# Linear attention and an MLP-Mixer on one core: the second half of w_ch2 goes behind batch 1 in the stream of loads

## The chip, the cores and the metric

The kernel runs on one core of a Trainium2 chip. TensorE multiplies matrices, VectorE and ScalarE move and combine elements, GpSimd here mostly issues loads and stores, and 16 DMA engines move the data. The metric is the time on the device in microseconds (us), the median of three runs. Before the change it is 423.5 us (422.79 to 423.52). The profile is of one execution of 423.1 us, whose span from the first to the last instruction is 421.2 us; all times within the profile count from the start of that span.

## The reference

```
k_proj = E @ k            v_proj = F @ v          per batch and head, 1024 -> 64 rows
attn   = softmax(q @ k_proj.T / 8) @ v_proj       -> x, 1024 x 512 per batch
u      = x + (relu(x.T @ w_tok1) @ w_tok2).T      w_tok1 1024 x 256, w_tok2 256 x 1024
out    = u + relu(u @ w_ch1) @ w_ch2              w_ch1 512 x 1536, w_ch2 1536 x 512
```

There are 8 batches, 8 heads of 64, and a sequence of 1024. Inputs and output are float32; the products run in bfloat16 with float32 sums.

## The kernel before

The two channel products hold most of the work. A batch is cut into two blocks of 512 rows, so there are 16 blocks j. For each block `up_set` (from line 1127) computes relu(u @ w_ch1) in three sets, and `down_block` (from line 1218) multiplies the result, G, with w_ch2. Both use a scheme of Winograd and Strassen: a product of 2 x 2 quarters takes seven quarter products in place of eight, numbered 1 to 7, at the price of sums and differences of quarters on VectorE. Products 1, 2, 3 and 5 use quarters of the weights; products 4, 6 and 7 use combined quarters (`combine`, line 441: four differences a piece, of which number 5 overwrites a quarter of the weights). For w_ch2 (`wc2_sb`, combined in `wT2`) there are two pieces, chunks 0 to 2 and chunks 3 to 5 of each half of the 1536 rows. Every product of a down block runs over all six chunks, so no down-projection can start until both pieces of its quarter are there.

An up set is 7 products of 4 matmuls of 256 columns (line 1144). Between them ScalarE copies a partial sum from one PSUM bank into the next (line 1187), keeps two intermediate sums (line 1172) and applies two relus (line 1166), and VectorE makes two sums with relu (line 1125) and the four sums of G for the down block (line 1180). A down block is 14 groups of 6 matmuls of 256 columns (line 1253), with one ScalarE copy (line 1309) and six VectorE additions (lines 1293 and 1303).

Beside blocks 2b and 2b+1 runs the front of batch b+1: projections of K and V (`kv_proj`, lines 484 and 487), transposes of K and Q, scores with an exp on ScalarE (lines 597 and 606), attention (line 620, with VectorE at 632 and 637), then the two token products. For batch 1 the projections and the transposes are done in two halves of four heads each, on TensorE. G and S have two buffers each, by the parity of the block; K, V and Q have one each, so batch b+1 is loaded as batch b's projections leave them.

The order of instructions is computed, not written. Each piece of work is a job with an engine, an estimated duration, its dependencies and a due time, `prio`. `Planner.plan` (line 83) runs through estimated time: of the jobs that can start first on an engine it takes the one with the earliest due time, gives PSUM banks to those that need them (the up-projections may hold 5 of 8 banks at once, the down-projections 3, the front 3), and notes a start `j.start` and a place `j.at`. At the end all jobs are sorted by `at` and written out in that order, and `pin` ties each engine to it. So each engine runs its instructions in a fixed order, and an instruction that waits holds up all that follow it on its engine.

The loads are one stream in the planner, as fast as 0.40 MB of float32 a microsecond. All are issued by GpSimd, and convert to bfloat16. A load is marked `early`: its place is not its planned start but the moment at which its buffer is free (line 172), so it's issued well ahead, and waits its turn in the DMA queue. The loads of the beginning get their due times from a counter, `first`, in the order of the program: K, V, Q of batch 0 with w_tok1 among them, w_tok2, the six pieces of w_ch1, the four of w_ch2 (lines 384 to 390), and then K, V, Q of batch 1 (lines 1454 to 1456). This line decides the place in the order:

```
j.at = est[j.n] if j.early else t
```

Of the kernel before, what the change touches and what calls it, by code (L numbers as in the profile page):

```python
# [11 lines left out]
ALU = mybir.AluOpType  # L12
ACT = mybir.ActivationFunctionType
EARLY = 12.0
WHOLE = 3
TWO = 2
SUMS = 60.0
# [27 lines left out]
class Planner:  # L45
# [37 lines left out]
    def plan(self):  # L83
# [7 lines left out]
        for g in self.groups:  # L91
            first = min(j.prio for j in g)
# [8 lines left out]
        est = {}  # L101

        def open_(j):
            est[j.n] = max((d.end + self.LAG[d.eng] if d.eng != j.eng else d.full for d in j.deps), default=0.0)
            can.setdefault(j.eng, []).append(j)
# [14 lines left out]
        def home(b, now):  # L120

            if held[b.stream] + b.span > self.caps[b.stream]:
                return None
            if b.span == 2:
                free2 = [
                    (max(now, bank_free[i], bank_free[i + 1]), i) for i in PAIRS[b.stream]
                    if bank_free[i] is not None and bank_free[i + 1] is not None
                ]
                return (*min(free2)[:1], 0, 0, min(free2)[1]) if free2 else None
            if b.stream in "UD" and turn[b.stream][0] is not b:  # L130
                return None
            best = None
            keep = [i for i in self.homes["U"] if clean[i] and bank_free[i] is not None]
            if all(clean[:5]):
                keep = []
            for i in self.homes[b.stream]:
                t = bank_free[i]
                if t is None or (b.seeded and not clean[i]):
                    continue
                if not b.seeded and clean[i] and keep and keep[-1] == keep[0] == i:  # L140
                    continue
                c = (max(now, t), clean[i], t, i)
                if best is None or c < best:
                    best = c
            return best

        while any(can.values()):
            pick = None
            for e, js in can.items():
                f = free.get(e, 0.0)  # L150
                cands = []
                for j in js:
                    t = max(f, est[j.n])
                    spot = None
                    if j.takes:
                        h = home(j.takes[0], t)
                        if h is None:
                            continue
                        t, spot = h[0], h[3]
                    cands.append((t, j.prio, j.n, j, spot))  # L160
                if not cands:
                    continue
                t0 = min(c[0] for c in cands) + 0.02
                c = min((c for c in cands if c[0] <= t0), key=lambda c: (c[1], c[2]))
                if pick is None or c[0] < pick[0]:
                    pick = c
            if pick is None:
                raise RuntimeError("no job can go on", [(j.eng, j.fn.__qualname__, j.prio) for js in can.values() for j in js][:20], held, bank_free)
            t, _, _, j, spot = pick
            can[j.eng].remove(j)  # L170
            j.start, j.end, j.full = t, t + j.lat, t + j.lat + 0.03
            j.at = est[j.n] if j.early else t
            free[j.eng] = t + j.occ
            if j.takes:
                b = j.takes[0]
                b.at = spot
                turn[b.stream].remove(b)
                held[b.stream] += b.span
                for i in range(spot, spot + b.span):
                    bank_free[i] = None  # L180
            for b in j.banks:
                left[id(b)] -= 1
                if not left[id(b)]:
                    held[b.stream] -= b.span
                    for i in range(b.at, b.at + b.span):
                        bank_free[i] = max(x.end for x in b.jobs) + 0.1
                        clean[i] = b.full
            order.append(j)
            for s in j.next:
                waiting[s.n] -= 1  # L190
                if not waiting[s.n]:
                    open_(s)
# [6 lines left out]
def kernel(  # L199
# [16 lines left out]
    B, H, S, D = q.shape  # L216
# [121 lines left out]
    def ld(mb, fn, **kw):  # L338
        t = mb / 0.40
        j = pl.add("DMA", t, t + 2.0, fn, **kw)  # L340
        j.early = True
        return j


    def dma(dst, src):
        return lambda: nc.gpsimd.dma_start(out=dst, in_=src)  # L346
# [8 lines left out]
    def load_heads(b, name, h, hn, due):  # L355
        dst, src = {"k": (k_sb, k), "v": (v_sb, v), "q": (q_sb, q)}[name]
        hs = slice(h, h + hn)
        return ld(
            0.262 * hn,
            dma(dst[:, hs], src[b, hs].rearrange("h (p si) d -> p h si d", p=P)),  # L360
            writes=[(name, i) for i in range(h, h + hn)], prio=due,
        )
    first = iter(range(-1000, 0))
# [10 lines left out]
    for m in range(SETS):  # L374
        cs = slice(m * cw, (m + 1) * cw)
        for ch in range(2):
# [5 lines left out]
                writes=[("w1", m, ch)], prio=next(first),  # L382
            )
    w2_v = moe_w_ch2.rearrange("(ch cc p) d -> p ch cc d", ch=2, p=P)
    for c in range(0, C2, 3):
        for ch in range(2):
            ld(
                0.786, dma(wc2_sb[:, ch, c : c + 3], w2_v[:, ch, c : c + 3]),
                writes=[("w2", ch, c // 3)], prio=next(first),
            )  # L390


    TU = 24.65
# [77 lines left out]
    def kv_proj(b, h0, hn, due, block=False):  # L471
        hs = slice(h0, h0 + hn)
        hk = slice(h0 % (H // 2), h0 % (H // 2) + hn)
        heads = range(h0, h0 + hn)
        bk = Bank(stream[0], full=False)

        def view():
            return bank(bk).rearrange("p (h d) -> p h d", d=D)

        def mm(lo, hi):  # L480
            t = view()
            for si in range(lo, hi):
                a, z = si == 0, si == NSI - 1
                nc.tensor.matmul(  # L484
                    t[0:KP, 0:hn], ET_sb[:, si, :], k_sb[:, hs, si, :], start=a, stop=z
                )
                nc.tensor.matmul(
                    t[KP : 2 * KP, 0:hn], FT_sb[:, si, :], v_sb[:, hs, si, :], start=a, stop=z
                )

        cols = hn * D
        reads = ["ET", "FT"] + [(n, h) for n in "kv" for h in heads]
        pl.add(
            "PE", 8 * max(cols, 128) / 2400 + 0.22, 8 * max(cols, 128) / 2400 + 0.22,
            lambda: mm(0, NSI), reads=reads, takes=[bk], prio=due,
            after=[("vb", i, h) for i in range(2) for h in heads],
        )
        src = [lambda: view()[0:KP, 0:hn], lambda: view()[KP : 2 * KP, 0:hn]]
        if block:
            k_to = [kb[i * KP : (i + 1) * KP, hs, i, :] for i in range(2)]  # L500
        else:
            k_to = [kp[:, hk, i, :] for i in range(2)]
        v_to = [vb[i * KP : (i + 1) * KP, hs, i, 0:D] for i in range(2)]

        def copy(to, n):
            return lambda: nc.scalar.copy(out=to, in_=src[n]())

        for i in range(2):
            act(cols, copy(k_to[i], 0), writes=[("kb" if block else "kp", i, h if block else h % (H // 2)) for h in heads], uses=[bk])
        for i in (1, 0):  # L510
            act(cols, copy(v_to[i], 1), writes=[("vb", i, h) for h in heads], uses=[bk])

    def k_transpose_dma():
        sp(
            2.5,
            lambda: nc.sync.dma_start_transpose(
                out=kT.rearrange("p h c k -> p h (c k)"), in_=kb.rearrange("p h r d -> p (h r d)")
            ),
            reads=[("kb", i, h) for i in range(2) for h in range(H)],
            writes=[("kT", i, h) for i in range(2) for h in range(H)], prio=None,  # L520
        )
# [887 lines left out]
    def front(b, begin, end):  # L1409
        units = []  # L1410

        def unit(cost, f):
            units.append((cost, f))

        hn = H // 2 if b == 1 else H
        for i in range(H // hn):
# [3 lines left out]
            else:  # L1420
                unit(1.9, lambda t: kv_proj(b, 0, H, t - EARLY, True))
                unit(0.0, lambda t: k_transpose_dma())
# [7 lines left out]
        for h in range(H):  # L1430
            if h + 2 < H:
                unit(0.4, lambda t, h=h: scores(h + 2, t))
            if b >= WHOLE:
                unit(0.5, lambda t, h=h: attend_whole(h, t))
# [18 lines left out]

    for hh in range(0, H, H // 2):
        for name in "kvq":
            load_heads(1, name, hh, H // 2, next(first))
    for b in range(B):
        for j in (2 * b, 2 * b + 1):
            s_sums(j)
# [67 lines left out]
```

The softmax here doesn't subtract the row's maximum and nothing guards it: scores larger than these inputs give would overflow.

## Time and profile before

| What | Value |
|---|---|
| median of 3 runs | 423.5 us |
| span in the profile | 421.2 us |
| TensorE busy | 412.1 us |
| VectorE busy | 348.0 us |
| ScalarE busy | 231.8 us |
| GpSimd busy | 66.2 us |
| first up-projection starts | 32.3 us |
| first down-projection starts | 44.1 us |
| first K and V projection of batch 1 | 47.3 us |

Busy times overlap, and each is to be read against the span. A busy TensorE is not yet one at its peak: the end of a matmul is modelled and reaches into the next one, so a gap is better read from the starts of two neighbours and the known pitch. In the lines of the profile, L1253 is a line of the kernel, PE is a matmul, PEld a weight load, DVE VectorE, ACT ScalarE and POOL GpSimd. "psum<-wc_sb,G" names what is written and read, with numbers of buffers left out: wc_sb stands for the weights of both channel products and wT for their combinations.

### The profile page before, as it was taken

How to read it: one execution, taken by the hardware profiler on the slowest of the kernel's cores; microseconds unless marked ns; L12 is line 12 of the kernel's file. 1: busy time of each engine (PE TensorE's matmuls, PEld its weight loads, DVE VectorE, ACT ScalarE, POOL GpSimd, SP SyncE). 2: the span in 40 equal slices, each digit the busy share in tenths (PEclk: the TensorE clock that was granted, in tenths of full speed). 3: DMA queues.
4: the chain of work that ended last, by engine and by line, in shares of the span. 5: the costliest groups of instructions: out<-in, count | busy, mean ns of one | idle time of the engine just before them, and what ended most of it. 6: DMA issues, size and time to landing. Idle time of an engine off the chain costs nothing.

```text
span 421.2 us, 9421 instructions
## 1 busy us (share of the span) xinstructions
PE 412.1 (98%) x3838; PEld 347.7 (83%) x3838; DVE 348.0 (83%) x747; ACT 231.8 (55%) x444; POOL 66.2 (16%) x104
## 2 busy tenths in 40 slices
PE   7999999999999999999999999999999999999996
PEld 3587877688788888888798888888898899988885
DVE  2359969679679798988889899898988798997685
ACT  1858884475636546564645556655646645354530
POOL 8453220022003030022103020212100000010110
PEclk9999999999999999999999999999999999999999
DMA  9999999996975989398974989999760501250223
GB/s 166 207 201 206 207 206 164 225 177 140 216 145 103 195 133 235 64 186 141 207 163 94 191 139 224 163 200 179 153 146 0 152 27 76 50 151 2 102 100 103
DMA packets 96668, 62.48 MB, mean 148 GB/s; under 512 B 62064, under 2 KB 92272, under 8 KB 96624
## 3 DMA queue, kind: packets, MB, share of 16 engines
q0 software_dynamic: 34944, 45.09, 54.5%
q1 hardware_dynamic: 61056, 16.00, 21.6%
q10 hardware_dynamic: 624, 0.79, 0.7%
q8 instruction: 30, 0.49, 0.5%
q14 instruction: 14, 0.11, 0.1%
HBM read 59.24 MB, written 16.78 MB: 180 GB/s over the span
## 4 chain that ended last, share of the span: by engine, by line
PE 91%; DVE 4%; ACT 2%; DMA 1%; issue 0%; DVEq 0%
PE psum L1253 34%; PE psum L1144 33%; PE psum L848 4%; PE psum L484 4%; PE psum L597 3%; PE psum L964 3%; PE psum L656 2%; DMA o<-in_F_dram 1%; PE psum L620 1%; DVE u L1071 1%; PE psum L736 1%; PE psum L687 1%; PE psum L581 1%; PE psum L405 1%; PE psum L711 1%; PE psum L1032 1%
## 5 line engine op out<-in xcount | busy, mean ns | idle before, releaser
L1253 PEld LDWEIGHTS <-G 128*128 128x128 bf16 x1344 | 130.6, 98 | 19.7 <-issue 1.5
L1253 PE MATMUL psum<-wc_sb,G 128*128 128x256 bf16 x768 | 102.5, 273 | 0.5 <-ACT psum L1309 0.2
L1166 ACT ACTIVATE G<-psum 128x512 bf16<-128x512 f32 x96 | 57.3, 600 | 56.0 <-PE psum L1144 55.4
L1144 PEld LDWEIGHTS <-wc_sb 128*128 128x128 bf16 x768 | 73.8, 98 | 10.9 <-issue 0.6
L1253 PE MATMUL psum<-wT,G 128*128 128x256 bf16 x576 | 77.7, 273 | 0.1
L1180 DVE TENSOR_TENSOR G<-G 128x512 bf16<-128x512 bf16 (+1 forms) x140 | 69.5, 516 | 1.0
L1144 PEld LDWEIGHTS <-wT 128*128 128x128 bf16 x576 | 55.7, 98 | 9.0 <-issue 1.2
L1144 PE MATMUL psum<-uT,wc_sb 128*128 128x256 bf16 x384 | 57.7, 273 | 0.2 <-ACT psum L1187 0.2
L1144 PE MATMUL psum<-S,wc_sb 128*128 128x256 bf16 x384 | 57.6, 273 | 0.1
L1144 PE MATMUL psum<-S,wT 128*128 128x256 bf16 x384 | 55.6, 273 | 0.4 <-DVE S L781 0.4
L1287 POOL DMA_DIRECT2D out_dram<-o x30 | 16.4, 548 | 240.2 <-DVE o L1293 125.6
L1125 DVE CUSTOM_DVE_ANT_0 G<-psum,ub 128x512 bf16<-128x512 f32 x48 | 32.9, 685 | 15.3 <-PE psum L1144 15.1
L1172 ACT COPY ua<-psum 128x512 f32<-128x512 f32 x48 | 28.2, 588 | 30.1 <-PE psum L1144 29.7
L606 ACT ACTIVATE a<-psum 128x512 bf16<-128x512 f32 x64 | 36.4, 602 | 12.4 <-PE psum L597 11.8
L1293 DVE TENSOR_TENSOR o<-psum,u 128x512 f32<-128x512 f32 x55 | 37.5, 683 | 6.4 <-PE psum L1253 6.3
L1187 ACT COPY psum<-psum 128x512 f32<-128x512 f32 x48 | 27.8, 580 | 18.9 <-DVE G L1125 9.9
L1125 DVE CUSTOM_DVE_ANT_0 G<-psum,ua 128x512 bf16<-128x512 f32 x48 | 32.7, 682 | 5.0 <-ACT ua L1172 4.6
L1172 ACT COPY ub<-psum 128x512 f32<-128x512 f32 x48 | 28.2, 588 | 7.0 <-PE psum L1144 6.3
L1144 PE MATMUL psum<-uT,wT 128*128 128x256 bf16 x192 | 28.8, 273 | 0.1
L673 DVE TENSOR_TENSOR x_sb<-psum,rdn 128x512 bf16<-128x512 f32 x40 | 27.4, 686 | 0.6
L597 PE MATMUL psum<-qT,kT 128*128 128x512 bf16 x64 | 21.5, 380 | 0.6 <-ACT kT L549 0.6
L346 POOL DMA_DIRECT2D v_sb<-in_v_dram x18 | 13.5, 749 | 50.7 <-DMA uT<-u 48.0
(108 smaller groups left out, 547.2 us busy)
## 6 DMA issues: line engine op xcount, KB each, us to landing
out_dram<-o POOLq DMA_DIRECT2D x30, 512.0 KB, 4.2
k_sb<-in_k_dram POOLq DMA_DIRECT2D x14, 512.0 KB, 8.5
v_sb<-in_v_dram POOLq DMA_DIRECT2D x14, 512.0 KB, 10.3
q_sb<-in_q_dram POOLq DMA_DIRECT2D x14, 512.0 KB, 9.9
wc_sb<-in_moe_w_ch_dram POOLq DMA_DIRECT2D x6, 256.0 KB, 12.3
wc_sb<-in_moe_w_ch_dram POOLq DMA_DIRECT2D x4, 384.0 KB, 12.3
k_sb<-in_k_dram POOLq DMA_DIRECT2D x4, 256.0 KB, 6.8
v_sb<-in_v_dram POOLq DMA_DIRECT2D x4, 256.0 KB, 7.3
```

The costliest lines, as they stand in the source:

```text
L484: nc.tensor.matmul(t[0:KP, 0:hn], ET_sb[:, si, :], k_sb[:, hs, si, :], start=a, stop=z)
L597: lambda: nc.tensor.matmul(bank(bk), kT[:, h].rearrange("p c k -> p (c k)"), qT[:, h].rearrange("p j s -> p (j s)"), start=True, stop=True,),
L606: lambda: nc.scalar.activation(out=a_t[h // 2 % 2][:, h % 2], in_=bank(bk), func=ACT.Exp, scale=scale),
L673: lambda: nc.vector.tensor_tensor(out=x_sb[:, :, h * D : (h + 1) * D].rearrange("p (n c) d -> p n c d", n=2), in0=view()[:, :, :, 0:D], in ...
L1125: nc.vector._custom_dve(TENSOR_ADD_SAT, out=out, in0=in0, in1=in1, s0=FMAX, s1=0.0)
L1144: nc.tensor.matmul(t[:, c, :], w1_of(n, dd, 2 * m + c), a_of(j, n, dd), start=(n in (1, 7) and c == 0 and dd == 0), stop=(c == 1 and dd == 1),
L1166: lambda: nc.scalar.activation(out=G[:, n, cs], in_=view(src), func=ACT.Relu),
L1172: 512, lambda: nc.scalar.copy(out=dst, in_=view("y")), writes=[(name, s % 2)],
L1180: 512 * len(both), lambda: f(out=G[:, n, c], in0=G[:, a, c], in1=G[:, b, c]), ps=False,
L1187: 512, lambda: nc.scalar.copy(out=view("y"), in_=view("x")), takes=[bk["y"]],
L1253: nc.tensor.matmul(to, G[:, G_OF[n], cc, t * P : (t + 1) * P], w2_of(n, cc), start=(n in opens and (t == 0 or alone) and cc == 0), stop=(c ...
L1293: 512, lambda: nc.vector.tensor_add(out=dst, in0=view(src), in1=u_of(sh, dh)),
```

## The change

The load of w_ch2 is cut in two in time. Chunks 0 to 2 stay where they were in the stream, behind w_ch1. Chunks 3 to 5 go behind all loads of batch 1. The aim is that K, V and Q of batch 1 come earlier, while the first down-projections, which need all six chunks, come later. To this end the loads get due times by hand: -700 for the first half of w_ch2, -400 to -358 for batch 1, -340 for the second half. The second half isn't `early` any more; it gets a place of 16 us (in the planner's time) ahead of its planned start, which puts it behind the loads of batch 1 in GpSimd's order too.

```diff
+W2_DUE = (-700, -340)
...
-            j.at = est[j.n] if j.early else t
+            j.at = est[j.n] if j.early else t - 16 if -500 < j.prio < -300 else t
...
     for c in range(0, C2, 3):
         for ch in range(2):
             ld(
                 0.786, dma(wc2_sb[:, ch, c : c + 3], w2_v[:, ch, c : c + 3]),
-                writes=[("w2", ch, c // 3)], prio=next(first),
-            )
+                writes=[("w2", ch, c // 3)], prio=W2_DUE[c // 3] + 0.1 * ch,
+            ).early = W2_DUE[c // 3] < -500
...
     for hh in range(0, H, H // 2):
         for name in "kvq":
-            load_heads(1, name, hh, H // 2, next(first))
+            load_heads(1, name, hh, H // 2, -400.0 + 10 * hh + "kvq".index(name))
```

## The prediction

> **What bounds the kernel now.** I read the page first (busy shares, slices, chain), then the list of waits of TensorE, then a table of stages, then the timelines of TensorE and GpSimd between 30 and 60 us.
>
> ```profile
> PE 412.1 (98%) x3838; PEld 347.7 (83%) x3838; DVE 348.0 (83%) x747; ACT 231.8 (55%) x444; POOL 66.2 (16%) x104
> ...
> DMA  9999999996975989398974989999760501250223
> ...
> PE 91%; DVE 4%; ACT 2%; DMA 1%; issue 0%; DVEq 0%
> ```
>
> TensorE is busy for 98% of the span and is 91% of the chain that ended last. The DMA engines are full in the first nine slices, some 95 us less a dip. So the time is TensorE's work plus TensorE's holes, and the change alters no product: it can only open or close holes. The list of waits of TensorE says how many there are to close.
>
> ```profile
> PE psum L433 <- DMA o<-in_F_dram: 1.5, 1, 1.5
> PE psum L405 <- DVE zero L309: 1.0, 1, 1.0
> PE psum L597 <- ACT kT L549: 0.6, 2, 0.4
> PE psum L1085 <- DVE u L1071: 0.5, 1, 0.5
> PE psum L1144 <- DVE S L781: 0.4, 1, 0.4
> PE psum L1253 <- ACT psum L1309: 0.2, 1, 0.2
> ```
>
> All but the last lie before 36 us. A busy share hides part of a hole, because the modelled ends of matmuls overlap (a product of 4 shows 0.60 us but the next starts 0.44 us later). So I also took the starts in TensorE's timeline and subtracted the pitch of each group (0.109 us a matmul of 256 columns, 0.22 of 512, 0.057 of 128): some 2.0 us of holes between 26 and 41 us, 0.8 from 40 to 60, 0.3 from 60 to 80, 0.8 from 80 to 100, and 2.6 from 100 to the end. About 0.2 to 0.3 us of these comes with each K and V projection, wherever it stands.
>
> The stage that matters is the one in which the first down-projections run:
>
> ```profile
> 40.00:44.00 4.00, 3.89 (x37) 3.40 (x35) 4.00 (x11) 3.51 (x7) 0.00 (x0) 1.00 1.24 206
> 44.00:47.00 3.00, 3.00 (x30) 2.68 (x29) 3.00 (x7) 2.38 (x6) 0.00 (x0) 1.00 1.24 207
> 47.00:52.00 5.00, 5.00 (x62) 4.03 (x60) 5.00 (x13) 3.88 (x9) 2.02 (x3) 1.00 1.24 207
> 52.00:56.00 4.00, 4.00 (x40) 3.13 (x39) 3.82 (x12) 3.64 (x7) 0.20 (x1) 1.00 1.24 206
> ```
>
> The columns are the stretch, its length, then busy time of PE, PEld, DVE, ACT and POOL, the clock, the DMA share and GB/s. From 44 to 56 us VectorE is full (11.8 of 12.0 us), ScalarE works 9.9 of 12.0, and the DMA runs at its limit. All four resources are near their ends at once, and TensorE has no hole only because it has a third kind of work:
>
> ```profile
> 44.14 0.82 PE L1253 MATMUL psum<-wc_sb,G 128*128 128x256 bf16 x6
> ...
> 46.11 0.82 PE L1253 MATMUL psum<-wc_sb,G 128*128 128x256 bf16 x6
> ...
> 51.43 0.82 PE L1253 MATMUL psum<-wT,G 128*128 128x256 bf16 x6
> ...
> 52.96 0.82 PE L1253 MATMUL psum<-wT,G 128*128 128x256 bf16 x6
> ...
> 53.83 0.82 PE L1253 MATMUL psum<-wT,G 128*128 128x256 bf16 x6
> ...
> 54.82 0.82 PE L1253 MATMUL psum<-wT,G 128*128 128x256 bf16 x6
> ```
>
> These six groups of down block 0 are 6 x 0.655 = 3.9 us of TensorE work, and they ask almost nothing of the other engines: one ScalarE copy (L1309, 46.96 us) and one VectorE add (L1293, 53.81 us) in those 12 us.
>
> **What the Trainium skill says.** "Perfetto Trace Analysis", Identifying the Most-Contended Engine, warns that matmul busy time is a poor measure of headroom; the trace agrees (0.60 us shown, 0.44 us pitch), hence the pitch count above. "PSUM — Partial Sum Buffer", Engine vs sequencer instructions, says that ScalarE and VectorE queues are strict FIFO and matmuls start in program order. The trace fits: at 35.93 us TensorE stands still for 0.41 us for one S sum, although other products follow. So an early place in the order that proves too early costs everything behind it. "DMA: Bandwidth & Descriptors", Issuing engines are not separate DMA queues, says that all issuers share the same 16 engines: what goes ahead in the stream pushes back the rest. Its Bandwidth section measures 425 GB/s for a large load; here 206 GB/s land as bf16, which is 412 GB/s of float32 read, so the stream has no speed in hand.
>
> **The change, part by part.**
>
> 1. *Where the loads land.* The half of w_ch2 that moves is two pieces of 384 KB (as landed): 2 x 0.393 MB / 206 GB/s = 3.8 us. A load of four heads is 0.524 MB, 2.5 us; six of them are 15.3 us. The first projection of batch 1 shows when its V has come:
>
> ```profile
> 47.29 0.30 PE L484 MATMUL psum<-k_sb,ET_sb 128*64 128x256 bf16 x1
> 47.49 0.27 PE L487 MATMUL psum<-v_sb,FT_sb 128*64 128x256 bf16 x1
> ...
> 50.09 1.07 PE L581 MATMUL psum<-ident,q_sb 128*128 128x128 bf16 x16
> ```
>
>    V's first matmul trails K's by 0.2 us, and the Q transposes follow 2.6 us later, one load's time: this front runs as its data lands. So K, V, Q of heads 0 to 3 land at about 44.9, 47.4, 49.9 now, and at 41.1, 43.6, 46.1 after; heads 4 to 7 at 48.7, 51.2, 53.7 instead of 3.8 us later; and the two pieces of w_ch2 at 55.7 and 57.6 instead of about 40.4 and 42.3. Batch 2's loads are behind all of these either way and don't move. The issue on GpSimd costs 0.74 us a load, before and after alike, and the batch 1 loads would be issued some 3 us sooner into buffers that the batch 0 projections (done at 23.4 us) and transposes (24.4 us) have left, so nothing new holds them: zero.
>
> 2. *The four W2 combinations of that half* (L444, 128x768, 0.55 us each, pitch 0.46) leave a full VectorE between 43 and 52 us and return after 57.6 us, where it has room (1.84 of 4.00 us from 56 to 60). That takes 4 x 0.46 = 1.8 us off VectorE in the stage. TensorE gains nothing from it directly, since it had no hole there.
>
> 3. *Down block 0.* Every product runs over all six chunks, so its first needs the piece that lands at 55.7, and the second (from combined weights) 57.6 + 0.46 = 58.1 us. The six groups, 3.9 us, lose their place in 44 to 56 us. What can fill it? Up-projections of block 1: 11 of its 21 products are done later than 58 us now, so there is plenty, but a set of seven (7 x 0.44 = 3.06 us) asks ScalarE for five passes at 0.49 pitch, 2.45 us, and VectorE for two add-relus, 1.2 us, and four sums, 1.34 us, which can wait. ScalarE's 2.1 spare us would carry at most 2.1 x 3.06 / 2.45 = 2.6 us of these. Or batch 1's attention, 3.8 us sooner: for four heads TensorE 1.1 + 0.2 + 0.9 + 0.9 + 0.9 = 4.0 us against ScalarE 1.35 + 0.73 + 1.93 + 1.96 = 6.0 us. Filling with that costs 1.5 us of ScalarE for 1 of TensorE, so 2.1 us carry 1.4. Thus 3.9 us of filler is lost, and 1.4 to 2.6 us is the most that replaces it: a hole of 1.3 to 2.5 us. Bounds: 0 if the 1.8 us freed on VectorE and the three free D banks let the up sets run denser than now, 3.9 if nothing fills. I take 1.7, below the middle, because up-projections stand ready from 36 us on and ScalarE idles here mostly in pieces of 1 us that they can use.
>
> 4. *Afterwards.* From 58 us on the postponed block is a stock of light work (9.2 us on TensorE), and batch 1's front is up to 3.8 us ahead. That can close the holes between 60 and 100 us, 1.1 us less 0.4 that the projections bring, so 0.7. It cannot give back the hole of step 3, because TensorE was full from 58 to 80 already.
>
>    Sum: + 1.7 - 0.7 = + 1.0 us: 423.5 + 1.0 = 424.5 us.
>
> **The rivals.** *A: fillers suffice.* No net change, 423.5. For it: 11 products in stock, banks free. Against: ScalarE is 4.96 of 5.00 busy from 50 to 55 us even now. *B: faster, 422.5.* VectorE's relief and the earlier front close what can be closed: 0.7 from step 4 and some 0.3 of the holes from 40 to 60, with none opened. For it: every piece of the front is now used as it lands. Against: TensorE is not waiting for the front. *C: nothing fills and the order frays*, all 3.9 us lost: 427.4. For it: the FIFO queues; against: the stock of ready work.
>
> **How the numbers follow.** Forecast 0.50, A 0.25, B 0.17, C 0.08. The predicted time is the forecast's. Within the forecast the hole runs from 1.3 to 2.5 and the return from 0 to 0.7, so + 0.6 to + 2.5; about a sixth of it lies under the 0.85 us that count as a difference. That part and most of A make 0.30 for no change; 0.50 slower (0.42 forecast and C's 0.08); B and a little of A 0.20 faster. The range 422.4 to 426.6 takes in B's value and the forecast and leaves out C and tails.
>
> **What would show it.** Step 1: the first L487 of 256 columns near 43.6 us. Step 2: no second round of 128x768 combinations before 57 us. Step 3: no L1253 before 55.5 us; ScalarE above 11 of 12 us from 44 to 56; TensorE's holes of one to two and a half us there, waiting for ScalarE or VectorE. Step 4: fewer holes from 60 to 100. The prediction is wrong if TensorE stays without holes from 44 to 56, or if it has other holes after 100 us that a different order closes or opens.

## The result and the profile after

The changed kernel takes 425.22 us, the median of 4 runs (424.94 to 425.33), against 423.51 before (422.79 to 424.21): ratio 1.0039, 95% interval 1.0022 to 1.0057, so 1.7 us slower. In a second comparison, beside other kernels, it was 425.71 against 423.56: 1.0049, 1.0036 to 1.0062.

The page after, the same rows as before:

```profile
PE 413.0 (98%) x3838; PEld 347.3 (82%) x3838; DVE 347.6 (82%) x747; ACT 231.5 (55%) x444; POOL 66.1 (16%) x104
...
DMA  9999999994994989497998996795972511250223
...
PE 80%; DVE 8%; ACT 5%; DMA 4%; issue 1%; POOL 1%; POOLq 0%; DVEq 0%; ACTq 0%
```

In the profiled execution the span grew from 421.2 to 423.4 us while the work of VectorE and ScalarE stayed as it was. The chain that ended last now passes more often through the other engines: TensorE has 80% of it, against 91% before. TensorE's last group starts at 418.87 us in place of 416.38. To see where these 2.5 us come in, I took the pitch count of the prediction on both traces (start of the next group less the start of this one, less the pitch of this one's matmuls):

| holes of TensorE, us | before | after |
|---|---|---|
| 0 to 40 us | 11.2 | 11.5 |
| 40 to 64 us | 1.0 | 2.6 |
| 64 to 80 us | 0.3 | 0.2 |
| 80 to 100 us | 0.8 | 1.0 |
| 100 us to the end | 2.8 | 3.3 |

The 0.3 us of the first row is not the change: the first up-projection starts at 32.33 us before and at 32.64 after, but at 32.36 in a second profile of the changed kernel. Most of the change is in the second row. Before, this stage is one row of the table of stages (stretch, length, busy PE, PEld, DVE, ACT, POOL, clock, DMA share, GB/s):

```profile
44.00:64.00 20.00, 20.00 (x213) 16.39 (x212) 16.72 (x45) 16.89 (x34) 4.44 (x6) 1.00 1.24 207
```

and after:

```profile
52.00:56.00 4.00, 4.00 (x53) 3.15 (x51) 3.82 (x12) 3.94 (x10) 1.48 (x2) 1.00 1.24 205
56.00:60.00 4.00, 3.78 (x34) 2.81 (x32) 2.38 (x9) 3.95 (x8) 0.74 (x1) 1.00 1.23 205
60.00:64.00 4.00, 3.72 (x36) 2.94 (x35) 3.93 (x13) 3.32 (x7) 0.00 (x0) 1.00 1.25 208
44.00:56.00 12.00, 11.95 (x135) 9.34 (x130) 11.35 (x29) 11.57 (x26) 3.74 (x5) 1.00 1.24 206
44.00:64.00 20.00, 19.45 (x200) 15.09 (x195) 17.67 (x49) 18.85 (x39) 4.48 (x6) 1.00 1.24 206
```

The fourth number after the length is ScalarE: 18.85 of 20 us, up from 16.89, and 3.95 of 4 from 56 to 60 us, where TensorE loses time. TensorE's timeline after shows the holes one by one, and where down block 0 (L1255 in this kernel) now begins:

```profile
56.66 0.82 PE L1255 MATMUL psum<-wc_sb,G 128*128 128x256 bf16 x6
...
58.08 0.82 PE L1255 MATMUL psum<-wc_sb,G 128*128 128x256 bf16 x6
58.82 0.39 PE L622 MATMUL psum<-vb,a 128*128 128x130 bf16 x4
59.32 0.38 PE L599 MATMUL psum<-qT,kT 128*128 128x512 bf16 x1
59.80 0.60 PE L1146 MATMUL psum<-S,wc_sb 128*128 128x256 bf16 x4
60.23 0.39 PE L622 MATMUL psum<-vb,a 128*128 128x130 bf16 x4
60.79 0.38 PE L599 MATMUL psum<-qT,kT 128*128 128x512 bf16 x1 [0.17 <-ACT a L608]
61.28 0.82 PE L1255 MATMUL psum<-wc_sb,G 128*128 128x256 bf16 x6
```

Four matmuls of 130 columns take 0.23 us, but 58.82 to 59.32 is 0.50; a score takes 0.22, but 59.32 to 59.80 is 0.48. From 58.8 to 61.3 us there are four holes of 0.26 to 0.33, 1.1 us together. ScalarE's timeline has the other side of them:

```profile
57.76 1.01 ACT L591 COPY qT<-psum 128x1024 bf16<-128x1024 bf16 x1
58.67 0.60 ACT L608 ACTIVATE a<-psum 128x512 bf16<-128x512 f32 x1
59.16 0.59 ACT L1174 COPY ua<-psum 128x512 f32<-128x512 f32 x1
59.62 0.63 ACT L1168 ACTIVATE G<-psum 128x512 bf16<-128x512 f32 x1
60.11 0.63 ACT L608 ACTIVATE a<-psum 128x512 bf16<-128x512 f32 x1
60.59 0.65 ACT L1311 COPY psum<-psum 128x512 f32<-128x512 f32 x1
61.10 0.64 ACT L1168 ACTIVATE G<-psum 128x512 bf16<-128x512 f32 x1
```

There is no pause between any two: Q copies, exps, the passes of the up sets, and in their midst the one copy of the down block (L1311). Each of the four holes ends some 0.05 us after one of these does: at 59.27 (an exp), 59.75 (a copy of an up set), 60.74 (an exp) and 61.24 us (the down block's copy, after which its third group starts at 61.28). So even the filler that has come back stands in ScalarE's queue.

### The profile page after: what moved, and what is told of

The parts are those of the page before. It is cut to its first block, busy times and chain, and to the rows that moved or that the text cites. A ratio compares the mean times of both kernels' runs of the same rounds, so it can differ in the third digit from the quotient of the medians.

```text
span 423.4 us, 9409 instructions
## 1 busy us (share of the span) xinstructions
PE 413.0 (98%) x3838; PEld 347.3 (82%) x3838; DVE 347.6 (82%) x747; ACT 231.5 (55%) x444; POOL 66.1 (16%) x104
## 4 chain that ended last, share of the span: by engine, by line
PE 80%; DVE 8%; ACT 5%; DMA 4%; issue 1%; POOL 1%; POOLq 0%; DVEq 0%; ACTq 0%
PE psum L1255 32%; PE psum L1146 29%; PE psum L850 4%; PE psum L966 3%; DMA q_sb<-in_q_dram 3%; PE psum L486 3%; PE psum L599 2%; PE psum L658 2%; DVE G L1127 2%; DMA v_sb<-in_v_dram 2%; DVE G L1182 1%; DVE u L1073 1%; ACT qT L591 1%; PE psum L713 1%; PE psum L689 1%
## 5 line engine op out<-in xcount | busy, mean ns | idle before, releaser
L1255 PEld LDWEIGHTS <-G 128*128 128x128 bf16 x1344 | 130.2, 98 | 20.1 <-issue 2.3
L1255 PE MATMUL psum<-wc_sb,G 128*128 128x256 bf16 x768 | 102.7, 273 | 0.8 <-DVE wait L1295 0.4
L1255 PE MATMUL psum<-wT,G 128*128 128x256 bf16 x576 | 77.7, 273 | 0.2
L1146 PEld LDWEIGHTS <-wT 128*128 128x128 bf16 x576 | 55.5, 98 | 9.4 <-issue 1.0
L1146 PE MATMUL psum<-S,wc_sb 128*128 128x256 bf16 x384 | 57.6, 273 | 0.2
```

What stands on the lines that cost most here:

```text
L1146: nc.tensor.matmul(t[:, c, :], w1_of(n, dd, 2 * m + c), a_of(j, n, dd), start=(n in (1, 7) and c == 0 and dd == 0), stop=(c == 1 and dd == 1),
L1255: nc.tensor.matmul(to, G[:, G_OF[n], cc, t * P : (t + 1) * P], w2_of(n, cc), start=(n in opens and (t == 0 or alone) and cc == 0), stop=(c ...
```

## The experiments

The theory was: moving the load makes down block 0 late, TensorE loses its light work between 44 and 56 us, and ScalarE can't carry enough of the other work. The rivals were that the early front of batch 1 itself crowds ScalarE, and that a reshuffled order loses time anywhere. Holes are from the pitch count. In the table, the times of before are those measured beside each kernel, and "holes" are of TensorE. They are of one execution each, the times are medians: e7, for one, ran between 425.63 and 430.11 us, and its profile is of 428.76. A dash marks a trace that lacks a dozen matmul records, where a missing record would be counted as a hole.

| kernel | us | before beside it | ratio (95%) | holes 40 to 64 | 64 to 100 | after 100 |
|---|---|---|---|---|---|---|
| before | | | | 1.0 | 1.0 | 2.8 |
| after | 425.22 | 423.51 | 1.0022 to 1.0057 | 2.6 | 1.2 | 3.3 |
| e2, down block 0 held | 428.35 | 423.44 | 1.0099 to 1.0134 | 2.7 | 0.6 | 5.7 |
| e3, half not loaded | 426.85 | 423.44 | 1.0058 to 1.0095 | 1.4 | 0.9 | 5.2 |
| e4, after without Q copies | 425.61 | 423.44 | 1.0037 to 1.0062 | 1.1 | 2.3 | 3.7 |
| e5, before without Q copies | 423.89 | 423.44 | 1.0002 to 1.0018 | 0.6 | 1.4 | 3.9 |
| e1, half way | 428.11 | 423.45 | 1.0091 to 1.0127 | 1.3 | 1.7 | 6.4 |
| e6, e3 with a clean start | 423.92 | 423.45 | 1.0002 to 1.0021 | 0.9 | 1.0 | 3.9 |
| e7, short hold | 427.45 | 423.45 | 1.0065 to 1.0126 | 1.2 | 0.6 | 8.1 |
| e8, e2 without Q copies | 426.50 | 423.45 | 1.0057 to 1.0112 | 0.9 | 3.4 | 3.0 |
| e9, after, Q copies on VectorE | 431.84 | 423.56 | 1.0176 to 1.0219 | - | - | - |
| e10, before, Q copies on VectorE | 429.83 | 423.56 | 1.0119 to 1.0169 | - | - | - |
| e11, one load later | 423.53 | 423.56 | 0.9991 to 1.0007 | - | - | - |

**e2: the late block without the moved load.**

```diff
-        product(1, 0)
+        opening[j] = product(1, 0)[0]
...
+    opening[0].deps.add(proj[1, H // 2])   # the second K and V projection of batch 1
     plan = pl.plan()
```

> The kernel before with its loads untouched; only down block 0 is held in the order until the second K and V projection of batch 1 is planned, so its first group starts near 56 us as after the change, while batch 1's front stays at its old time. Theory (the lost filler): TensorE loses the six groups of 44 to 56 us and ScalarE cannot carry enough in their place: 1.0 to 2.5 us slower than before, with holes of 1 us or more before 65 us. Rival (the early front crowds ScalarE): within 0.5 us of before, since the front is not early here. Rival (an order reshuffled later): any small difference, with its holes after 65 us.

Measured: 4.9 us slower. From 40 to 60 us it has 2.7 us of holes against 0.9 before, 1.8 more, and 2.1 of the 2.7 lie between 52 and 56 us, where ScalarE has no time left (the fourth number after the length). The waits of TensorE from 44 to 64 us in e2 all name ScalarE:

```profile
52.00:56.00 4.00, 2.91 (x20) 1.49 (x18) 3.69 (x13) 4.00 (x8) 0.22 (x1) 1.00 1.24 204
...
PE psum L621 <- ACT a L607: 0.4, 2, 0.2
PE psum L598 <- ACT qT L590: 0.3, 1, 0.3
```

So a late down block opens ScalarE's holes with every load where it was. The other 3 us of e2 come later (the row's last column), which the theory had not foreseen; of that below.

**e3 and e6: the early front without the late block.** The second half of w_ch2 is not loaded; zeros stand in for it, so the result is wrong, but every product and sum is still done. In e3 GpSimd set the zeros and held up the first loads by 1.4 us, which spoils its time; e6 has them set by VectorE.

```diff
+    nc.vector.memset(wc2_sb[:, :, 3:6], 0.0)    # e3: nc.gpsimd.memset
...
-        for ch in range(2):
+        for ch in range(2 if c == 0 else 0):
...
-            cols=3 * DH, name="W2", n=c, reads=[("w2", 0, c), ("w2", 1, c)],
+            cols=3 * DH, name="W2", n=c, reads=[("w2", 0, 0), ("w2", 1, 0)],
...
-            w = [("w2", {1: 0, 2: 1, 3: 1}[n], c) for c in range(2)]
+            w = [("w2", {1: 0, 2: 1, 3: 1}[n], 0)]
```

> The kernel after, but the second half of w_ch2 is not loaded at all: it is zeros set at the start, so half of each down-projection multiplies by zero; every product, combination and sum is still done. Batch 1 then lands 3.8 us earlier and down block 0 still starts near 44 us. Theory (the lost filler): no loss, 0 to 1 us faster than before. Rival (the early front crowds ScalarE): 1 us or more slower than before, as after. Rival (an order reshuffled later): no clear side.

> The run without a load of the second half of w_ch2 again, with the zeros set by VectorE at the start in place of GpSimd, which had held up the first loads by 1.4 us there. Half of each down-projection multiplies by zero; all other work is done. Theory (lost filler): with down block 0 at its old time the early front alone opens no holes: 40 to 100 us has 2.0 to 2.5 us of holes as before, and what is slower than before lies in the one wait for batch 3's V near 109 us (1.2 us in the first such run), so 0 to 1.5 us slower in all. Rival (the early front crowds ScalarE): 3.5 us or more of holes from 40 to 100 us.

Measured: e3 3.4 us slower, of which 1.4 are the start and 0.9 a wait for batch 3's V at 109 us; e6 0.5 us slower. Its stage:

```profile
44.00:64.00 20.00, 20.00 (x216) 16.50 (x213) 17.78 (x52) 18.36 (x37) 4.44 (x6) 1.00 1.24 207
```

ScalarE is as busy as in the changed kernel (18.36 against 18.85 of 20), batch 1 is as early, and TensorE is full: its holes from 40 to 100 us are 1.9 us, against 2.1 before. So the early front by itself is harmless, and it also gains nothing: that rival falls. Down block 0 is not quite at its old time here, though: its first group starts at 46.46 us, and three of its groups start before 56 us in place of six. That these three are missed without a hole is a second finding.

**e4, e5 and e8: less work for ScalarE.** The four copies of batch 1's transposed Q are left out, in the kernel after, before, and in e2; batch 1's scores then use batch 0's Q.

```diff
+        skip = due > -18 and stream[0] == "F"    # batch 1
         pe(2 * NJ, 128, mm, reads=[("q", 2 * hp), ("q", 2 * hp + 1)], takes=[bk], prio=due)
+        if skip:
+            return
         act(
             1024, lambda: nc.scalar.copy(out=qT[:, 2 * hp : 2 * hp + 2], in_=view()),
```

> The kernel after without ScalarE's four copies of the transposed Q of batch 1 (3.7 us of ScalarE); batch 1's scores use batch 0's Q. Theory (ScalarE is what can't carry the replacement): the holes of TensorE between 56 and 62 us close, and this comes within 0.5 us of the kernel before with the same copies left out; 1.0 to 1.7 us faster than after. Rival (VectorE or the order): still about 1.5 us slower than before without the copies.

> The kernel before without the same four copies of the transposed Q of batch 1; batch 1's scores use batch 0's Q. It is the base for the run after without the copies. All theories: within 0.5 us of before, since TensorE had no hole there for ScalarE to close.

> The kernel before with down block 0 held until the second K and V projection of batch 1, and without ScalarE's four copies of the transposed Q of batch 1 (its scores use batch 0's Q). Theory (ScalarE can't carry the replacement): the cluster of holes at 52 to 56 us of the long hold closes, 40 to 60 us falls from 2.7 to 1.2 us of holes or less. Rival (VectorE or the order): 2.2 us or more remain there.

Measured, from 44 to 64 us, first e4 and then e8 (e2 has 18.91 us of TensorE and 18.28 of ScalarE there):

```profile
44.00:64.00 20.00, 19.97 (x219) 16.57 (x217) 18.47 (x56) 15.80 (x34) 4.48 (x6) 1.00 1.24 206
```

```profile
44.00:64.00 20.00, 19.89 (x215) 16.25 (x213) 18.33 (x53) 16.27 (x36) 4.44 (x6) 1.00 1.24 207
```

The holes close: e8 has 0.9 us from 40 to 60 us where e2 has 2.7, and in e4 the row from 58.8 to 61.3 is gone. VectorE is busier there than in e2 and in the kernel after, and TensorE is full all the same, so VectorE is not what held it. But the time did not follow. e4 stays 1.7 us above e5, where I expected 0.5 at most. By the table, 0.5 us of it still lies between 40 and 64 us, and 0.9 from 64 to 100: the projection of batch 2 comes up sooner, at 69.3 us in place of 71.4 in the changed kernel, and waits for its load.

```profile
PE psum L489 <- DMA v_sb<-in_v_dram: 0.9, 1, 0.9
```

And e8 stands 2.7 us at 88 us, for batch 2's Q from the DMA transpose:

```profile
PE psum L601 <- DMA qT<-q_sb: 2.7, 1, 2.7
```

**e9 and e10: two of the copies on VectorE.** All is computed, in the kernel after and before. This was the try at a version that beats both.

```diff
-        act(
-            1024, lambda: nc.scalar.copy(out=qT[:, 2 * hp : 2 * hp + 2], in_=view()),
+        by = (dve, nc.vector.tensor_copy) if stream[0] == "F" and hp >= 2 else (act, nc.scalar.copy)
+        by[0](
+            1024, lambda: by[1](out=qT[:, 2 * hp : 2 * hp + 2], in_=view()),
```

> The kernel after with the two copies of the transposed Q of heads 4 to 7 of batch 1 on VectorE in place of ScalarE, which has room there (2.4 of 4.0 us busy from 56 to 60). All is computed. Theory (ScalarE can't carry the replacement): the row of holes from 58.8 to 61.3 us (1.1 us) shrinks by half or more; 0.3 to 1.0 us faster than after if nothing is lost later in the order. Rival (VectorE or the order): no change there, or new holes of the same size.

> The kernel before with the same two copies on VectorE. All theories: within 0.5 us of before, because TensorE has no hole there to close; if it beats before, it is the best version.

Measured: where the changed kernel had its row of holes, e9 has none:

```profile
56.00:60.00 4.00, 4.00 (x39) 3.42 (x39) 2.96 (x8) 3.45 (x8) 0.74 (x1) 1.00 1.24 206
60.00:64.00 4.00, 4.00 (x40) 3.45 (x39) 3.99 (x14) 2.53 (x5) 0.00 (x0) 1.00 1.24 207
```

That is the theory's mark, with the full computation. But e9 is 8.3 us slower than before, 6.1 slower than the changed kernel, and e10 is 6.3 slower than before, both far from what I expected; e9 waits 3.0 us for the transposed Q at 92 us and in many small waits for VectorE to the end, e10 1.5 us for G's sums at 85 us and 1.6 for output additions. Neither is a better version.

**e1, e7 and e11: how much later.** e1 puts the second half behind K, V, Q of heads 0 to 3; e11 behind their K alone; e7 holds the block, loads untouched, until the Q transposes of heads 0 to 3.

```diff
-W2_DUE = (-700, -340)
+W2_DUE = (-700, -380)      # e11: -399.5, placed with K of heads 0 to 3
...
-            j.at = est[j.n] if j.early else t - 16 if -500 < j.prio < -300 else t
+            j.at = est[j.n] if j.early else t - 22 if -500 < j.prio < -300 else t
```

```diff
+    opening[0].deps.add(turns[1][1])     # e7
```

> The kernel after with the second half of w_ch2 halfway: behind K, V, Q of heads 0 to 3 of batch 1, ahead of heads 4 to 7. It lands near 48 and 50 us, so down block 0 opens near 48 to 50 us, and only the first half of the front is early. Theory (lost filler): TensorE's holes from 40 to 100 us lie between those of before (2.05 us) and after (3.8 us); 0.3 to 1.2 us slower than before. Rival (an order reshuffled): anything from 1 us faster to 2 us slower, with its holes at other places than 44 to 62 us.

> The kernel before, loads untouched, with down block 0 held only until the Q transposes of heads 0 to 3 of batch 1, near 51 us instead of 56. Two of the six groups lose their place, so theory (lost filler): less than half of the long hold's extra holes from 40 to 60 us (1.8 us there), 0 to 0.8 us. Rival (an order reshuffled): no relation to the length of the hold.

> The kernel after with the second half of w_ch2 only one load later than before: behind K of heads 0 to 3 of batch 1, ahead of their V. It lands near 42.9 and 44.8 us, and down block 0 still opens near 44 us, so no filler is lost. Theory (lost filler): holes from 40 to 64 us within 0.4 us of before, and within 0.5 us in all, unless the order later on is altered. Rival (an order reshuffled): more than 1 us slower, with holes after 64 us, as in the halfway run.

Measured: the holes from 40 to 64 us grow with the delay, but not in proportion (1.0 before, 1.2 and 1.3 with the block delayed by part of it, 2.6 and 2.7 with the full delay). e7 keeps two of the six groups before 56 us, not four as I had expected: its first starts at 51.69 us and its third at 57.50. e1 keeps five, and e6 above three. So up to four of the groups were missed for 0.3 us at most; the holes came only where all six were gone and ScalarE had all its work. One load later costs nothing, 423.53 against 423.56. The times of e1 and e7 do not follow: 4.7 and 4.0 us slower, where 1.2 was the most that the theory gave e1, and e7 has hardly a hole more in the stage. In e7 the largest part is the first of these waits:

```profile
PE psum L488 <- DMA v_sb<-in_v_dram: 2.4, 1, 2.4
PE psum L966 <- DVE a L996: 0.7, 1, 0.7
```

It is the projection of batch 3, at 109.6 us; the last part of its V may only be loaded behind the transpose of batch 1's second block. e2 (1.7 us), e3 (0.9) and e5 (0.6) wait at the same place, the changed kernel does not. e1 waits there for 0.3 us alone; what it loses after 64 us is in holes of up to 0.9 us, most of them behind VectorE or ScalarE, spread over the later batches. So the rival of the reshuffled order is real too, only elsewhere: once the block moves, all that follows is planned anew, and where the new order meets a load or a transpose too early, TensorE stood for up to 3.0 us. Which estimate of the planner is off was not tried.

**The changed kernel once more**, beside the last three:

> The changed kernel itself once more, beside the next three. All theories: 1.0 to 2.2 us slower than before; its holes from 40 to 64 us again 1 us or more above those of before.

Measured: 425.71 against 423.56, 2.1 us, with the same row of holes from 59.2 to 61.7 us. The sum from 40 to 64 us can't be given, because 14 matmul records are missing from this trace.

## Why the prediction was right, and where it was off

I forecast 424.5 us, in a range of 422.4 to 426.6; it is 425.22. Of the steps:

1. *Where the loads land*: right. The first matmul of V for batch 1 starts at 43.64 us (43.6 forecast) and the first down group at 56.66 (not before 55.5). That the order of the loads costs nothing by itself fits e11, where one load changes its place (0.9991 to 1.0007).
2. *The combinations*: right. Their second round starts at 58.69 us (after 57.6), and no gain came of it.
3. *The hole*: the cause is right, the place is not, and the size is right in part by luck. I set 1.7 us, between 1.3 and 2.5, and 1.6 more were measured from 40 to 64 us. ScalarE as the limit is shown by e4, e8 and e9, and the late block as what brings it there by e2. But I placed the hole between 44 and 56 us. There ScalarE is at 11.57 of 12.0 as forecast, yet TensorE is only some 0.5 us worse: of the 3.9 us of filler some 3.4 were replaced, where I had allowed for 1.4 to 2.6, and e6 and e7 missed three and four of the groups almost for nothing. That TensorE had no hole "only because" of these groups was therefore too strong, and my own sign of being wrong, no holes from 44 to 56 us, was not far off. The other 1.1 us come from 56 to 62 us, where I had counted on TensorE being full from 58 on: there ScalarE has the rest of the attention and the up sets to work off, and the down block is back, but its third group hangs on a copy in ScalarE's queue. I had not followed that copy, though I had cited "PSUM — Partial Sum Buffer", Engine vs sequencer instructions, for just this: a strict FIFO, in which the copy that ends at 61.24 us stood behind exps and up passes.
4. *The return*: wrong. I took 0.7 us of holes to close between 60 and 100 us. None closed: from 64 to 100 us there are 0.2 us more than before, and 0.5 more after 100. This is the term that was mis-sized: with 0 in its place the sum is 423.5 + 1.7 = 425.2. The later holes were not of the kind that more stock cures: the two largest up to 100 us, 0.5 us each at 84 and 99 us, wait for ScalarE's copy and VectorE's addition ahead of a down group, and similar ones, of 0.4 and 0.2 us, were there before at 82 and 97.

Rival A, that the fillers suffice, nearly holds from 44 to 56 us and fails from 56. Rival B, that the earlier front gains, falls with e6. Rival C, that nothing fills and the order frays, did not happen: 1.6 of the 3.9 us were lost. A fraying of another kind, far behind the stage, cost e1, e2 and e7 some 3 to 4.4 us; 0.08 was low for such a thing in a change that shifts a planned order, and nothing in the profile of before shows it. That the changed kernel was spared is luck: 3 us more would have put it outside the range.

## What to carry to other kernels

When TensorE is full, ask what each product asks of the other engines: here products that need few passes to clear them kept TensorE going where ScalarE was near its end, and a load that delayed all of them cost time although other products stood ready. Losing a part of them cost almost nothing, so look for the point at which the last is gone. Follow the one small copy that the returning work needs, for it queues behind the backlog. And in an order computed from estimates, judge a variant by its holes stage by stage: a local gain or loss of 1 us was drowned several times here by a wait elsewhere.

## What was not expected

The size of that last effect. Moving two copies from ScalarE to VectorE closed the row of holes in e9 and still cost 6 us in all, in the kernel after as in the kernel before; leaving four copies out of the kernel before, less work in an order planned anew, made it 0.5 us slower (1.0002 to 1.0018). In e7, e8 and e9 the longest wait is for a DMA transpose or a load tied to one: 2.4, 2.7 and 3.0 us. In e10 it is for VectorE, 1.5 us for G's sums and 1.6 for output additions, and e9 has waits for VectorE besides; why so little more work on VectorE costs so much was not tried.
